# Staging two chunks of the values' weights in another tile at the start of the second layer

## The chip, the cores and the metric

The kernel runs on one core of one Trainium2 chip. The metric is the device time of one execution in microseconds; the median of several runs is compared. Engines are named as in the profile: PE (TensorE, matrix products), DVE (VectorE), ACT (ScalarE), POOL (GpSimd) and SP, which issues all transfers here.

## The reference

Two layers, each of a linear attention and a dense part, with the same weights in both layers. All data is float32, x has 2048 rows of 640.

```
x = A_x
x = x + attention(layernorm(x), wqkv, w_phi, wo)
x = x + mish_mlp(layernorm(x), w1, b1, w2)
x = x + attention(layernorm(x), wqkv, w_phi, wo)
x = x + mish_mlp(layernorm(x), w1, b1, w2)

attention: q, k, v = split(x @ wqkv)            # 32 heads of 20
           pq, pk = q @ w_phi, k @ w_phi        # per head
           phi(p) = [softmax(p), softmax(-p)]
           kv, z  = phi_k^T v, sum of phi_k
           (phi_q kv) / (phi_q z + 1e-6) @ wo
mish_mlp:  h = x @ w1 + b1                      # 640 -> 1536
           (h * tanh(softplus(h))) @ w2         # 1536 -> 640
```

## The kernel before

**Products.** Every float32 operand of a large product is split into a high and a low part in a rounded float32 format, and each product is done three times: high by high, high by low, low by high. For a weight the split is `split` (lines 136 to 138) or `make_parts` (156 to 159): ACT copies the raw chunk into the high part, and DVE or POOL subtracts that from the raw chunk for the low part. A raw chunk is 128 rows of the weight, so a weight of 640 rows has five chunks, `k` = 0 to 4.

**Stages.** The 2048 rows go in eight blocks of 256, `b` = 0 to 7. Each layer has three stages. `attend_first` projects keys (`k0`, `k1`), values (`v0`, `v1`) and queries (`q0`, `q1`) of both 128-row halves of a block with `project_half` (line 364), and sums the keys' features times the values into one PSUM tile (line 436). `attend_second` applies the sums to the queries and projects with `wo` (also line 364). `dense` does the two products with Mish between them: `hidden` (line 759), `mish` (772 to 785, which ends with the high and low parts `ol` of the activation), `contract` (line 801, two steps behind `hidden`), and `end` (819 to 829: adds the residual, writes the rows out, normalises them for the next layer and spills the transposed rows to DRAM as `n_d`, line 337).

**The switch of layers.** In layer one's `dense`, the last pass of the loop (`i == len(steps) - 1`, line 870) calls `load_v_weights` (183 to 188) for layer two: the columns `D` to `2 * D` of the tiles `r1h`, `r1l` get the values' weights again, from the input `wv`. The same tiles held `w1` until the last `hidden`. The keys' weights, folded with `w_phi` in layer one and kept in DRAM (`wp_d`), are fetched into the other columns (line 200), and the queries' weights into `r2h`, `r2l` (line 194). Just ahead of it the loop takes the first block of layer two, `nxt`: its transposed rows were loaded by `load_turned` (line 345) into two tiles of values and one tile of rows, and `nxt.all()` (lines 305 and 306) splits them into `xth` and `xtl`. In layer two `b == 0` has the order `v0`, `k0`, `k1`, `v1`, `q0`, `q1`. The values of the first block go into single PSUM tiles (`one`, four in all, of which one holds the sum over the keys), two for each half of 128 rows; keys and queries go into the double tiles `mm` (two in all), which `contract` holds till `end`.

**Tiles between.** A raw chunk of `wv` goes through a tile that belongs to something else at other times. `fetch_v` (line 177) takes for `k` = 0 and 1 a tile of normalised rows (`xn`, tag of four buffers), for 2 and 3 a tile of values (`v`, two buffers), and for 4 a tile of the Mish steps (`big`, five buffers). The tile of a block's rows (`xt`, made by `x_tile`, two buffers, 128 by 2 by 640) holds a block of the residual stream: `dense` fetches the next block's rows into one while the other is in use, and the last use of one is in `end`. In the second layer `attend_first` has no use for it.

**Order.** Except where a part is written out by hand, a planner sets the order of the instructions on each engine's queue at build time, from times that it reckons and from the program's order; on the chip each queue then runs in that order, and waits where an input is not there. `issue_after` queues what is in it behind a given instruction of the same engine: so the splits of `load_v_weights` stand on ACT behind the last exponential of `mish`, and `act` (line 123) queues each of its copies behind the one before it in the program. The splits of the output weights for layer two (`make_five`, line 208, its transfers at line 151, its copies at line 158) are not held in that chain.

Of the kernel before, what the change touches and what calls it, by code (L numbers as in the profile page):

```python
# [16 lines left out]
P = 128  # L17
S = 2048
D = 640
# [22 lines left out]
def kernel(  # L42
# [13 lines left out]
    nc = tc.nc  # L56
# [17 lines left out]
    def x_tile():  # L74
        return work.tile([P, BT, D], F32, tag="x", name="xt", bufs=2)
# [17 lines left out]
    two = const.tile([P, 1], F32, name="two")  # L93
# [42 lines left out]
    def split(hi, lo, st):  # L136
        nc.scalar.activation(hi, st, AF.Copy)
        nc.vector.tensor_tensor(lo, st, hi.bitcast(F32), op=ALU.subtract)
# [26 lines left out]
    def r1_pair(k):  # L165
        return tuple(wts.tile([P, F], F32R, tag=f"r1{s}{k}", name=f"r1{s}{k}") for s in "hl")
# [10 lines left out]
    def fetch_v(k):  # L177

        st = (row_tile, row_tile, v_tile, v_tile, big_tile)[k]()[:, :D]
        nc.sync.dma_start(st, wv[k * P:(k + 1) * P, :])  # L180
        return st

    def load_v_weights():

        ws = [r1_pair(k) for k in range(KD)]
        for k in range(KD):
            split(ws[k][0][:, D:2 * D], ws[k][1][:, D:2 * D], fetch_v(k))
        return ws

    def load_q_weights():  # L190
# [554 lines left out]
    def dense(x_src, x_dst, w1s, w2s, first, last):  # L745
# [97 lines left out]
        for i in range(len(steps) + SKEW):  # L843
# [26 lines left out]
            if i == len(steps) - 1 and not last:  # L870
                with tc.issue_after(exps[0]):
                    kv_ws = load_v_weights()
# [90 lines left out]
```

## Time and profile before

| | us |
|---|---|
| median of three runs | 1378.19 |
| lowest, highest | 1376.71, 1378.69 |
| the profiled execution's own time | 1376.81 |
| its span, from the first to the last instruction | 1375.0 |
| PE, weight loads busy | 1362.1, 1349.8 |
| DVE, ACT, POOL busy | 1073.3, 581.3, 441.0 |
| mean granted clock of PE | 0.999 |

The profile is of one execution. A row of the timeline gives start and length in us, engine (SPq is SP's queue of transfers), line, operation, tile written and tiles read, and in brackets the idle time of the engine before it and what ended it; `x3` says that three instructions stand in the row. Weight loads and products of PE overlap, and a product's end is modelled. Names like `in_wv` and `in_wo` are the inputs in DRAM.

### The profile page before, as it was taken

The page shows a single profiled execution, that of the slowest core. Times are in us where ns is not written, and L with a number is a line of the kernel's source. Part 1 is how long each engine was busy: PE and PEld are TensorE (multiplying, and loading weights), DVE is VectorE, ACT ScalarE, POOL GpSimd, SP SyncE. Part 2 cuts the span into 40 slices and gives each one's busy share as a digit, 9 for nine tenths or more (in the row PEclk, how much of TensorE's full clock was granted, in tenths as well). Part 3 has the DMA queues.
Part 4 walks back from the last instruction along what each step waited for, and adds up shares of the span by engine and source line. Part 5 has one row for each costly group of instructions (what it writes and reads, how often), then busy time and mean ns, then how long its engine had stood idle before and what let it go on. Part 6 is the DMA issues. An engine that isn't in the chain of part 4 may idle for free.

```text
span 1375.0 us, 30860 instructions
## 1 busy us (share of the span) xinstructions
PE 1362.1 (99%) x12896; PEld 1349.8 (98%) x12896; DVE 1073.3 (78%) x1822; ACT 581.3 (42%) x970; POOL 441.0 (32%) x334
## 2 busy tenths in 40 slices
PE   9999999999999999999999999999999999999998
PEld 8999999999999999999999999999999999999998
DVE  5898877886688887788769899988678776677775
ACT  4344443222454545545444334332235444454443
POOL 1345553354322222122235434444242111111112
PEclk9999999999999999999999999999999999999999
DMA  9443424788614442244473433368975221333200
GB/s 337 148 95 62 75 40 96 204 242 292 224 55 97 116 105 77 59 107 99 141 245 77 85 59 64 67 132 270 285 253 151 77 59 41 94 97 96 69 29 20
DMA packets 350469, 169.85 MB, mean 124 GB/s; under 512 B 287209, under 2 KB 323801, under 8 KB 350329
## 3 DMA queue, kind: packets, MB, share of 16 engines
q1 hardware_dynamic: 350329, 167.88, 45.2%
q8 instruction: 101, 1.65, 0.5%
q14 instruction: 39, 0.32, 0.1%
HBM read 104.92 MB, written 62.91 MB: 122 GB/s over the span
## 4 chain that ended last, share of the span: by engine, by line
PE 96%; DMA 1%; DVE 1%; ACT 0%; issue 0%; DVEq 0%; SPq 0%
PE mm L364 29%; PE one L759 24%; PE mm L801 24%; PE one L364 12%; PE mm L637 3%; PE one L300 2%; PE one L436 2%; DMA v<-in_wv 1%; DMA r1l<-wp_d 0%; DVE r1l L251 0%; DVE bn L270 0%; ACT xn L129 0%; DVE r L397 0%; DVE xt L811 0%; ACT r L129 0%
## 5 line engine op out<-in xcount | busy, mean ns | idle before, releaser
L801 PE MATMUL mm<-r2h,ol 128*128 128x320 f32 x1280 | 305.0, 309 | 0.0
L785 POOL TENSOR_TENSOR ol<-big,ol 128x512 fp32r<-128x512 f32 (+1 forms) x98 | 129.9, 1326 | 483.7 <-ACT ol L784 409.3
L759 PE MATMUL one<-xtl,r1h 128*128 128x256 f32 x960 | 268.2, 279 | 0.0
L759 PE MATMUL one<-xth,r1l 128*128 128x256 f32 x960 | 268.0, 279 | 0.0
L759 PE MATMUL one<-xth,r1h 128*128 128x256 f32 x960 | 265.9, 279 | 0.0
L801 PEld LDWEIGHTS mm<-r2h,ol 128*128 128x128 f32 x1280 | 219.2, 188 | 0.3 <-ACT ol L784 0.3
L801 PE MATMUL mm<-r2l,ol 128*128 128x320 f32 x640 | 197.3, 309 | 0.0
L364 PE MATMUL mm<-r1h,xth 128*128 128x320 f32 x600 | 187.6, 313 | 1.6 <-DVE r1l L251 1.6
L364 PE MATMUL mm<-r1l,xth 128*128 128x320 f32 x600 | 185.8, 310 | 0.0
L364 PE MATMUL mm<-r1h,xtl 128*128 128x320 f32 x600 | 185.6, 310 | 0.0
L759 PEld LDWEIGHTS one<-xtl,r1h 128*128 128x128 f32 x960 | 180.4, 188 | 0.0
L759 PEld LDWEIGHTS one<-xth,r1l 128*128 128x128 f32 x960 | 180.4, 188 | 0.0
L759 PEld LDWEIGHTS one<-xth,r1h 128*128 128x128 f32 x960 | 179.6, 188 | 0.0
L774 DVE TENSOR_SCALAR big<-big 128x512 f32<-128x512 f32 (+1 forms) x98 | 57.1, 583 | 110.0 <-ACT big L772 109.8
L399 POOL TENSOR_TENSOR r<-r,r 128x1280 f32<-128x1280 f32 x32 | 77.7, 2429 | 156.4 <-DVE r L398 141.8
L801 PEld LDWEIGHTS mm<-r2l,ol 128*128 128x128 f32 x640 | 120.2, 188 | 0.0
L776 ACT ACTIVATE big<-big,two 128x512 f32<-128x512 f32 (+1 forms) x98 | 70.1, 716 | 116.1 <-DVE big L775 116.0
L772 ACT ACTIVATE big<-one,b1s 128x256 f32<-128x256 f32 x192 | 80.9, 468 | 89.0 <-PE one L759 88.5
L784 ACT ACTIVATE ol<-big 128x512 fp32r<-128x512 f32 (+1 forms) x98 | 60.9, 622 | 136.0 <-DVE big L783 135.9
L364 PEld LDWEIGHTS mm<-r1h,xth 128*128 128x128 f32 x600 | 112.8, 188 | 2.6 <-DVE r1l L251 1.8
L364 PEld LDWEIGHTS mm<-r1h,xtl 128*128 128x128 f32 x600 | 112.7, 188 | 0.2
L364 PEld LDWEIGHTS mm<-r1l,xth 128*128 128x128 f32 x600 | 112.8, 188 | 0.0
(133 smaller groups left out, 3119.9 us busy)
## 6 DMA issues: line engine op xcount, KB each, us to landing
e_d<-r SPq DMA_DIRECT2D x128, 160.0 KB, 4.0
big<-e_d SPq DMA_DIRECT2D x32, 640.0 KB, 7.6
x_d<-xt SPq DMA_DIRECT2D x23, 640.0 KB, 3.9
xt<-x_d SPq DMA_DIRECT2D x22, 640.0 KB, 5.5
n_d<-xn SPq DMA_DIRECT2D x176, 80.0 KB, 2.2
xt<-in_x SPq DMA_DIRECT2D x16, 640.0 KB, 4.4
xn<-x_d SPq DMA_DIRECT2D x28, 320.0 KB, 4.4
v<-n_d SPq DMA_DIRECT2D x30, 256.0 KB, 3.1
```

Source lines behind the costliest of these rows:

```text
L300: nc.tensor.transpose(ps[:, c, t * P:(t + 1) * P], self.rows[t][:, (c0 + c) * P:(c0 + c + 1) * P], ident)
L364: nc.tensor.matmul(ps[:, :HC], a[:, sl], r, start=(k == 0 and n == 0), stop=(k == KD - 1 and n == 2))
L399: nc.gpsimd.tensor_tensor(eg, eg, r.unsqueeze(2).to_broadcast([P, 2 * H, DH]), op=ALU.mult)
L436: nc.tensor.matmul(kva[32 * j:32 * j + DH + 1, 40 * r:40 * r + 40], v[:, (DH + 1) * h:(DH + 1) * (h + 1)], e[:, 40 * h:40 * h + 40], start ...
L637: nc.tensor.matmul(po[64 * q:64 * q + 64, c, GW * j:GW * j + w], phs[g][:n, s0:s0 + 64], kvb[:n, g, :w], start=True, stop=True)
L759: nc.tensor.matmul(ph[:, j, :], l, r, start=(n == 0), stop=(n == 3 * KD - 1))
L772: exps[0] = nc.scalar.activation(part(ta, 0)[:, j - js.start], ph[:, j, :], AF.Exp, bias=b1s[:, 2 * pr + j:2 * pr + j + 1]).ins
L774: nc.vector.tensor_scalar_min(e, e, E_CAP)
L776: nc.scalar.activation(r, n, AF.Ln, bias=two)
L784: nc.scalar.activation(ah[:, js], n, AF.Copy)
L785: nc.gpsimd.tensor_tensor(al[:, js], n, ah[:, js].bitcast(F32), op=ALU.subtract)
L801: nc.tensor.matmul(pys[t][:, c, :HC], l[:, j, sl], r, start=(f == 0 and n == 0), stop=(f == KF - 1 and n == 2))
```

## The change

For the second layer, chunks 2 and 3 of `wv` are fetched into the two halves of one tile of a block's rows, and split from there. Chunks 0, 1 and 4 go through the same tiles as before. The first layer, which calls `fetch_v` itself, is unchanged.

```diff
     def load_v_weights():
 
         ws = [r1_pair(k) for k in range(KD)]
+        two = x_tile()
         for k in range(KD):
-            split(ws[k][0][:, D:2 * D], ws[k][1][:, D:2 * D], fetch_v(k))
+            if k in (2, 3):
+                st = two[:, k - 2]
+                nc.sync.dma_start(st, wv[k * P:(k + 1) * P, :])
+            else:
+                st = fetch_v(k)
+            split(ws[k][0][:, D:2 * D], ws[k][1][:, D:2 * D], st)
         return ws
```

## The prediction

> **What bounds the kernel now.** I read the page first (busy times, then the chain that ended last), then the list of who waited for whom on TensorE, and then only the switch from layer one to layer two, around 690 us, because that is where the edited function runs: the chain within that window, the busy times there, and the timelines of the queues.
>
> ```profile
> PE 1362.1 (99%) x12896; PEld 1349.8 (98%) x12896; DVE 1073.3 (78%) x1822; ACT 581.3 (42%) x970; POOL 441.0 (32%) x334
> ...
> PE 96%; DMA 1%; DVE 1%; ACT 0%; issue 0%; DVEq 0%; SPq 0%
> ```
>
> TensorE is the bound: 1362.1 of 1375.0 us, and 96% of the chain. Everything that can be won in the whole span is 12.9 us of idle TensorE. In the list of its waits (total, times, longest, in us) one row belongs to this change:
>
> ```profile
> PE one L364 <- ACT r1h L137: 0.9, 1, 0.9
> ```
>
> A projection (L364) waits for a cast of line 137, which is `split` of a chunk of the values' weights, once. The chain through the switch shows which chunk (start, length, what):
>
> ```profile
> 695.81 7.14 DMA v<-in_wv
> ...
> 702.97 0.74 ACT r1h L137
> ...
> 703.76 0.71 PE one L364 x3
> 704.47 1.17 PE mm L801 x8
> 705.64 3.52 PE one L364 x24
> 709.16 8.80 PE mm L364 x60
> 717.96 2.20 PE one L364 x15
> ```
>
> Chunk 2 goes through a tile of values: its transfer starts at 695.81, lands after 7.14 us, is cast in 0.74, and TensorE starts at 703.76. After that TensorE is never late until the second attention: one product takes 8.80/60 = 0.147 us, and 60 and 15 follow at that pace.
>
> ```profile
> 690.00:697.00 7.00, 7.00 (x51) 7.00 (x50) 5.10 (x13) 5.32 (x12) 1.29 (x1) 1.00 0.95 336
> 696.00:700.00 4.00, 4.00 (x29) 4.00 (x28) 3.12 (x8) 1.89 (x5) 2.03 (x1) 1.00 1.03 404
> 697.00:705.00 8.00, 7.05 (x46) 6.53 (x45) 4.87 (x10) 3.02 (x6) 2.76 (x2) 1.00 0.79 295
> 705.00:718.00 13.00, 13.00 (x91) 13.00 (x90) 5.56 (x13) 5.74 (x11) 7.31 (x7) 1.00 0.52 172
> ```
>
> Those are busy times by stretch (length, then PE, PEld, DVE, ACT, POOL, granted clock, DMA share, GB/s). Only the stretch from 697 to 705 has a hole: 8.00 - 7.05 = 0.95 us of products, 8.00 - 6.53 = 1.47 us of weight loads. The clock is 1.00 throughout, so it plays no part.
>
> **The change part by part.** Two transfers of 320 KB, two casts and two subtractions stay as they are; only the tile between them differs. Nothing is added to the work of any engine. What moves is when the two transfers may start, and with them the order of four instructions. The transfer queue, SP:
>
> ```profile
> 668.54 0.34 SPq L825 DMA_DIRECT2D x_d<-xt  x1
> ...
> 674.99 7.01 SPq L337 DMA_DIRECT2D n_d<-xn  x8
> ...
> 683.57 0.43 SPq L180 DMA_DIRECT2D xn<-in_wv  x1
> ...
> 695.81 2.90 SPq L180 DMA_DIRECT2D v<-in_wv  x2
> ```
>
> *Start of the transfers.* The two v transfers stand behind the two casts and subtractions (`step`, L305 and L306) that empty the tiles of values into `xth` and `xtl`; these run after the last exponentials of layer one. The free tile of rows is the one of block 6. It is last read by its write-out at 668.54 and by its normalising on ACT (next fence, 672.85, 1.72 long, so to 674.57). Block 7's own rows stand in the other. So the transfers may start from about 674.6, behind the spill of eight pieces, which ends at 682.00, if the planner puts that first: 13.8 us earlier than 695.81 at the worst. SP waits for nothing new; behind them on SP would be the spill and the reloads of the queries' weights, each by 2 x 0.43 = 0.86 us, and the queries come last in the block.
>
> *The transfers themselves.* The DMA engines are full already (0.95 and 1.03 of them busy). One chunk of 327,680 bytes at the 404 GB/s of the fullest stretch is 0.81 us. Two go ahead of all that is queued from 684 on, so the fifth chunk, the one in `big`, would land up to 1.62 us later: it was there at 699.06, and would be at 700.7. With a cast of 0.74 and a subtraction of 0.82 it would be ready at 702.3, against 705.4 (703.74 + 1.63, below) for the last of the v chunks now. So the set of five is complete 3.1 us earlier, and the fifth chunk is late next. TensorE begins the values at 697.39:
>
> ```profile
> 697.39 0.60 PE L364 MATMUL one<-r1h,xth 128*128 128x320 f32 x3
> ...
> 717.80 0.31 PE L364 MATMUL one<-r1h,xth 128*128 128x320 f32 x1
> ```
>
> From there it has 36 products on chunks 0 to 3 (four chunks, three products, the three halves of values that have a PSUM tile) before it must touch the fifth, 5.3 us; with half of the last 24 products of the dense stage between them (1.8 us) that is 704.5, so it does not wait for the fifth. The Trainium skill, "DMA: Bandwidth & Descriptors", section Queues, rings and completion order, says that each DMA engine consumes its descriptors in ring order; that rule speaks against the change, and by it the 1.62 us of delay falls on the fifth chunk in full. No run here shows the new order yet.
>
> *Casts and subtractions.* On ACT:
>
> ```profile
> 672.85 1.72 ACT L129 ACTIVATE xn<-xt,stats 128x640 f32<-128x640 f32 x2
> ...
> 699.06 0.74 ACT L137 ACTIVATE r1h<-big 128x640 fp32r<-128x640 f32 x1 [1.89 <-DMA big<-in_wv]
> ...
> 714.26 0.74 ACT L158 ACTIVATE r2h<-raw 128x640 fp32r<-128x640 f32 x1 [3.90 <-DMA raw<-in_wo]
> 714.90 1.73 ACT L129 ACTIVATE xn<-xt,stats 128x640 f32<-128x640 f32 x2
> ...
> 716.65 0.74 ACT L129 ACTIVATE v<-one 128x320 f32<-128x320 f32 x2
> ...
> 734.18 0.74 ACT L158 ACTIVATE r2h<-xn 128x640 fp32r<-128x640 f32 x1 [4.46 <-DMA xn<-in_wo]
> ```
>
> The hole of 1.89 us ahead of 699.06 holds the two casts (2 x 0.74 = 1.48), so they cost ACT nothing if they fall there. The two subtractions have no such place (DVE's timeline from 701 on, and the row of POOL's in the same time):
>
> ```profile
> 701.03 0.43 DVE L783 SCALAR_TENSOR_TENSOR big<-big 128x256 f32<-128x256 f32 x1
> 703.74 1.63 DVE L138 TENSOR_TENSOR r1l<-v,r1h 128x640 fp32r<-128x640 f32 x2 [2.28 <-ACT r1h L137]
> 701.99 0.73 POOL L785 TENSOR_TENSOR ol<-big,ol 128x256 fp32r<-128x256 f32 x1 [2.36 <-ACT ol L784]
> ```
>
> They now stand after L783, the last DVE step of the dense stage; put ahead of it they delay that stage's last `ol` by 0 to 1.63 us. It is ready at 702.72 now (701.99 + 0.73); its last eight products ran only from 704.47 behind the late chunk, so 1.75 us of cover is there, and I take nothing for it.
>
> *The sum.* The wait of line 364 goes. Lower end 0.78 us: next in line is the PSUM slot for the fourth half of the values. The copy that frees it starts at 716.65 and its first half ends about 717.02, and TensorE's 15 products for that half come at 717.80 (second row of TensorE's timeline above); if the copy stays where it is, TensorE can come only 0.78 us earlier. Upper end 1.47 us, the weight loads' hole. The hole of products, 0.95, lies between. I take the middle, 1.1 us. [...]
>
> The profiled execution took 1376.81 us, 1.81 around its span of 1375.0, and 1.38 under the 1378.19 of the runs' median. So the same kernel profiled should show 1376.81 - 1.1 = 1375.7, and the median of runs 1378.19 - 1.1 = **1377.1 us**, 0.08% less. About 0.2% (2.76 us) is what a measurement of this kernel can tell from no change, so this is no change.
>
> **The rivals.**
>
> *Given back (1378.2 us).* The planner puts the two subtractions and casts ahead of the last steps of the dense stage, the last `ol` comes up to 1.63 us later, and TensorE waits for that instead of for the chunk; or the values' copy on ACT, which `act` holds behind the normalising of block 7, keeps its place and eats the rest. For it: DVE is 5.10 of 7.00 busy before 697, without a hole of 1.63. Against: 1.75 us of cover. The gain of 1.1 goes to nothing or little.
>
> *Slower (1381.5 us).* One mechanism, on ACT's queue. The copy of the values at 716.65 stands in program order behind the normalising of block 7 at 714.90, and that behind a cast of the output weights at 714.26 which waited 3.90 us for its transfer. These casts (L158) are free for the planner to place; it places them by reckoned times, and the change moves those times. One more of them in front, the fifth, costs as at 734.18: 4.46 of waiting and 0.74 of cast, 5.20 us. The slack before TensorE notices is 0.78. So the last half of values starts 5.20 - 0.78 = 4.4 us later than now if the queue in front of the copy keeps its place, and 3.3 us later if it comes the 1.1 us earlier with the end of the dense stage. I take the second: 1378.19 + 3.3 = 1381.5. It decides as soon as the copy ends over 0.78 us later. For it: the slack is that small, and the queues in front are in order. Against: the order after 705 follows from the dense stage's end, which hardly moves. A second step displaced would double it.
>
> *Faster by over 0.2%.* It would take 2.76 us of idle TensorE, and from 690 to 718 there are at most 1.47 us; the rest of the 12.9 lies in stretches that the edited function does not run in. Only a new order in the attention behind could bring it: about 1375 us.
>
> *It does not do what it says:* the tile of block 6 is held longer than I read, and the transfers stay near 695.8. Then nothing changes, and it counts with "given back".
>
> **How the numbers follow.** My forecast 0.38, given back 0.22, slower 0.34, faster 0.06. The first two lie within 0.2%: 0.60. I give the slower case that much because four in-order queues are laid out anew by reckoned times around a slack of 0.78 us, where the gain is limited to 1.47. The forecast's own range is 1378.19 - 1.47 = 1376.7 to 1378.19 - 0.78 = 1377.4. The range for 8 in 10 starts 1 us under that for the noise of the median (the three runs spread over 1.98), at 1375.7, and must take in most of the slower case: its price and a good part of a second step, to 1383.0.
>
> **What would show it.** Right: in the profile after, the transfers into `xt` from `in_wv` start before 684; the row of L364 waiting for the cast of L137 is gone or names `big`; TensorE's 60 products of L364 into `mm` start at about 708 instead of 709.16; weight loads from 697 to 705 are over 7.5 of 8.00; and the `v<-one` copy comes at 716 or before. Wrong: a wait of TensorE of over 1 us on `v<-one` or on `ol` between 697 and 725; a cast of L158 with a long wait for `in_wo` standing newly before the values' copy; or a difference in a stretch that the change cannot reach.

## The result, and the profile after

The changed kernel takes 1380.31 us (median of 22 runs, 1378.15 to 1384.43) against 1377.82 us for the kernel before (22 runs, 1376.62 to 1380.38). The ratio is 1.0019 [1.0013, 1.0025]: slower by 0.19%, 2.5 us between the medians. The forecast was 1377.1. The profiled execution took 1380.52 us, its span is 1378.7; both lie 3.7 us above those of before. Line numbers behind the edited function are 6 higher than before (line 364 is 370, 783 is 789, 306 is 312).

From the page, and from the list of TensorE's waits (total, times, longest, in us):

```profile
PE 1363.5 (99%) x12896; PEld 1351.0 (98%) x12896; DVE 1075.1 (78%) x1822; ACT 580.7 (42%) x970; POOL 442.9 (32%) x334
...
PE one L306 <- issue: 1.8, 1, 1.8
PE one L370 <- ACT v L129: 1.6, 1, 1.6
...
PE mm L370 <- DVE xtl L312: 1.0, 2, 0.7
```

The wait of 0.9 us for the cast of line 137 is gone, as forecast. In its place stand a wait for the copy of the values and two waits for `xtl`, the low part of a block's turned rows. Neither row is in the list of before. (The first row belongs to the start of the second attention, near 936 us; before, the wait there is 0.7 us.) The stretches that the prediction showed (length, PE, PEld, DVE, ACT, POOL, granted clock, DMA share, GB/s):

```profile
690.00:697.00 7.00, 7.00 (x51) 7.00 (x50) 5.22 (x13) 5.47 (x11) 1.27 (x1) 1.00 1.03 399
...
697.00:705.00 8.00, 8.00 (x56) 8.00 (x56) 4.96 (x9) 2.33 (x6) 3.29 (x2) 1.00 0.75 278
705.00:718.00 13.00, 11.63 (x78) 11.10 (x76) 4.29 (x11) 4.49 (x7) 7.34 (x8) 1.00 0.49 168
```

From 697 to 705 the hole is closed: 8.00 of weight loads where there were 6.53. The next stretch, full before, has a hole of 1.37 us of products and 1.90 us of weight loads. Timelines of TensorE, SP, ACT, DVE and POOL there (start, length, engine, line, operation, tiles; in brackets the idle time before and what ended it):

```profile
705.49 0.31 PE L370 MATMUL one<-r1h,xtl 128*128 128x320 f32 x1
705.64 0.31 PE L807 MATMUL mm<-r2h,ol 128*128 128x320 f32 x1
...
707.25 0.31 PE L807 MATMUL mm<-r2h,ol 128*128 128x320 f32 x1
707.89 0.41 PE L370 MATMUL mm<-r1h,xth 128*128 128x320 f32 x1 [0.33 <-DVE xt L825]
...
674.84 0.36 SPq L190 DMA_DIRECT2D xt<-in_wv  x1
...
683.54 0.53 SPq L190 DMA_DIRECT2D xt<-in_wv  x1
...
694.92 0.33 SPq L180 DMA_DIRECT2D big<-in_wv  x1
...
702.60 5.65 SPq L151 DMA_DIRECT2D raw<-in_wo  x3
...
701.49 0.74 ACT L137 ACTIVATE r1h<-big 128x640 fp32r<-128x640 f32 x1 [3.32 <-DMA big<-in_wv]
703.91 0.42 ACT L790 ACTIVATE ol<-big 128x256 fp32r<-128x256 f32 x1 [1.69 <-DVE big L789]
...
715.73 0.74 ACT L158 ACTIVATE r2h<-raw 128x640 fp32r<-128x640 f32 x1 [3.46 <-DMA raw<-in_wo]
716.37 1.72 ACT L129 ACTIVATE xn<-xt,stats 128x640 f32<-128x640 f32 x2
...
718.12 0.74 ACT L129 ACTIVATE v<-one 128x320 f32<-128x320 f32 x2
...
697.56 1.54 DVE L138 TENSOR_TENSOR r1l<-xt,r1h 128x640 fp32r<-128x640 f32 x2
...
699.96 0.41 DVE L787 SCALAR_TENSOR_TENSOR big<-big 128x256 f32<-128x256 f32 x1
702.26 0.83 DVE L138 TENSOR_TENSOR r1l<-big,r1h 128x640 fp32r<-128x640 f32 x1 [1.89 <-ACT r1h L137]
703.00 0.42 DVE L788 SCALAR_TENSOR_TENSOR big<-big 128x256 f32<-128x256 f32 x1
703.45 0.42 DVE L789 SCALAR_TENSOR_TENSOR big<-big 128x256 f32<-128x256 f32 x1
...
704.41 0.74 POOL L791 TENSOR_TENSOR ol<-big,ol 128x256 fp32r<-128x256 f32 x1 [3.43 <-ACT ol L790]
```

Read TensorE's rows first. Before the change, its last eight products of the dense stage ran from 704.47 to 705.64. Now the last twelve run from 705.64 to 707.56. Counted from the last product of `hidden` in each profile (690.24 before, 690.12 after), the stage ends at 17.44 us instead of 15.40, 2.0 us later. TensorE does not wait for that: up to 707.56 no row from 697 on has a wait in brackets. Its queue, which the planner lays out like the others, has another order. Before, 21 products of the values stood ahead of the last eight products of the dense stage; now 45 do.

DVE's rows show that the activation is late as well. The two subtractions of the moved chunks (1.54 us) stand ahead of the last three steps of Mish, lines 787 to 789. Between 787 and 788 stands the subtraction of the fifth chunk, as it stood between 781 and 782 before:

```profile
699.84 0.82 DVE L138 TENSOR_TENSOR r1l<-big,r1h 128x640 fp32r<-128x640 f32 x1 [0.81 <-ACT r1h L137]
```

Then DVE waited 0.81 us for it. Now the chunk's transfer is issued at 694.92 instead of 692.30, its cast comes at 701.49 instead of 699.06, and DVE stands idle for it for 1.89 us with the last two Mish steps queued behind. The last `ol` is ready at 704.41 + 0.74 = 705.15 instead of 702.72. But TensorE takes it up only at 705.64, so this lateness does not hold TensorE up. In five more profiles with the same place of the last twelve products (e2, e4, e10, e11 and e15 below), `ol` is ready 0.7 to 1.8 us before they start, and they start 15.51 us after the last of `hidden` in all of them.

With the last product of the dense stage the whole end of the layer moves. SP issues three transfers of the output weights from 702.60 on and stands 9.1 us in all for products of the dense stage (`SPq L151 <- PE mm L807`; 6.6 before), which free the tiles; the row of the three ends at 708.25 instead of 706.33. Four casts of the output weights stand on ACT ahead of the normalising, in both profiles. The last of them comes at 715.73 instead of 714.26, the normalising at 716.37 instead of 714.90 and, in ACT's order behind that, the copy of the values at 718.12 instead of 716.65: from the last of `hidden`, 1.6 us later. TensorE goes on 0.47 us after the start of that copy (718.59), so the slack before was 717.80 - 716.65 - 0.47 = 0.68 us, where the prediction had 0.78, and 0.9 us are lost. TensorE is 1.4 us earlier than before at 703, waits 0.33 us at 707.56 for the residual that frees `mm`, and then 1.6 us for the copy.

The second loss is 70 us further on, in the first block of layer two, where the edited function does not run. The write-out of the second query tile (SP, line 448 or 454), ACT's copy of a later query projection into the slot that it frees, the DVE step that waits for this copy, and the last `xtl` of the next block. Before, then after:

```profile
753.66 3.77 SPq L448 DMA_DIRECT2D e_d<-r  x4
...
760.33 0.71 ACT L129 ACTIVATE r<-mm 128x640 f32<-128x640 f32 x1 [4.72 <-DMA e_d<-r]
...
761.07 1.54 DVE L388 TENSOR_REDUCE m<-r 128x32 f32<-128x640 f32 x2 [0.23 <-ACT r L129]
...
784.70 1.50 DVE L306 TENSOR_TENSOR xtl<-xn,xth 128x256 fp32r<-128x256 f32 x1
```

```profile
754.67 4.46 SPq L454 DMA_DIRECT2D e_d<-r  x4
...
762.82 0.71 ACT L129 ACTIVATE r<-mm 128x640 f32<-128x640 f32 x1 [4.77 <-DMA e_d<-r]
...
763.55 0.82 DVE L394 TENSOR_REDUCE m<-r 128x32 f32<-128x640 f32 x1 [3.34 <-ACT r L129]
...
787.70 1.49 DVE L312 TENSOR_TENSOR xtl<-xn,xth 128x256 fp32r<-128x256 f32 x1
```

The copy waits for the landing of a write to DRAM. It comes 2.49 us later, DVE idles 3.34 us for it in one piece, and `xtl` starts 3.00 us later and is ready at 789.19. That is past the point where TensorE wants it. Besides being shifted by the switch, block 0's steps stand in a new order: the planner, reckoning with other times, put both keys' maxima first on DVE, and on POOL the subtraction of the first query's maxima (line 395) ahead of the multiplication of the first key's features (line 405). TensorE's order of products in this block differs too. Differences in the queues are confined to the switch and this block.

One table follows TensorE through all of it. It gives how much later (+) or earlier (-) than in the profile of before TensorE begins the same product, counted from the last product of `hidden` in layer one, which removes what executions differ by before the switch (-1.1 to +1.6 us). The columns are times in the profile of before; the experiments' names are those below. The next to last column is the start of ACT's copy behind the write-out, counted from the same product (70.09 before); the last, the total of TensorE's waits for `xtl`.

| profile | 703 | 725 | 780 | 830 | 945 | copy at | `xtl` |
|---|---|---|---|---|---|---|---|
| after | -1.38 | +1.01 | +0.68 | +2.22 | +3.88 | 72.69 | 1.0 |
| e10 (after) | -1.38 | +0.95 | +0.62 | +2.15 | +3.13 | 72.95 | 1.0 |
| e11 (after) | -1.38 | +0.91 | +0.58 | +2.20 | +4.03 | 72.86 | 1.0 |
| e1 | +0.08 | +0.08 | -0.25 | -0.25 | +0.18 | 69.89 | 0 |
| e8 | +0.14 | +0.15 | -0.18 | -0.18 | +0.49 | 69.84 | 0 |
| e12 | -0.36 | -0.36 | -0.69 | +1.04 | +3.02 | 71.79 | 1.2 |
| e7 | +0.22 | +0.37 | +0.04 | +2.09 | +3.21 | 72.63 | 1.5 |
| e2 | -1.38 | +1.06 | +1.06 | +1.06 | +1.60 | 71.55 | 0 |
| e4 | -1.38 | +1.08 | +1.09 | +1.08 | +3.10 | 71.88 | 0 |
| e6 | -1.38 | +0.07 | +0.07 | +0.07 | +0.64 | 70.66 | 0 |
| e3 | -1.38 | -0.81 | -0.79 | -0.63 | +0.55 | 69.75 | 0 |
| e5 | -1.38 | -0.77 | -0.76 | +0.80 | +4.03 | 71.51 | 1.0 |
| e13 | +0.54 | +0.54 | +0.54 | +0.54 | +1.28 | 67.94 | 0 |
| e14 | +0.38 | +0.38 | +0.05 | +0.05 | +0.82 | 67.46 | 0 |
| e15 | -1.38 | +3.24 | +2.91 | +2.91 | +3.67 | 70.79 | 0 |

Two rows hold something else besides. In e15 the granted clock is 0.84, 0.50 and 0.80 in the three stretches of 2 us from 720 on, and in e5 it is 0.57 from 937 to 941. The share that is missing, times the length, gives 1.7 us each time (an estimate), in the columns 725 and later for e15 and in the column 945 for e5.

### The profile page after: what moved, and what is told of

It is laid out like the page before. It is cut to its first block, busy times and chain, and to the rows that moved or that the text cites. A ratio compares the mean times of both kernels' runs of the same rounds, so it can differ in the third digit from the quotient of the medians.

```text
span 1378.7 us, 30858 instructions
## 1 busy us (share of the span) xinstructions
PE 1363.5 (99%) x12896; PEld 1351.0 (98%) x12896; DVE 1075.1 (78%) x1822; ACT 580.7 (42%) x970; POOL 442.9 (32%) x334
## 5 line engine op out<-in xcount | busy, mean ns | idle before, releaser
L807 PE MATMUL mm<-r2h,ol 128*128 128x320 f32 x1280 | 304.9, 309 | 0.0
L807 PEld LDWEIGHTS mm<-r2h,ol 128*128 128x128 f32 x1280 | 219.2, 188 | 0.0
L807 PE MATMUL mm<-r2l,ol 128*128 128x320 f32 x640 | 197.3, 309 | 0.0
L807 PEld LDWEIGHTS mm<-r2l,ol 128*128 128x128 f32 x640 | 120.2, 188 | 0.0
```

What stands on the lines that cost most here:

```text
L807: nc.tensor.matmul(pys[t][:, c, :HC], l[:, j, sl], r, start=(f == 0 and n == 0), stop=(f == KF - 1 and n == 2))
```

## The experiments

Two theories stood at the start. *Switch*: the loss is the subtractions and the late fifth chunk ahead of Mish's last steps, which make the dense stage end late. *Order*: the loss is the new order of block 0's steps on DVE and POOL. Where a kernel needs a given order of those steps, they are chained with dependencies that add no wait: the names below are maxima (M), minima (N), subtractions (S, D), sums (R), reciprocals (C), multiplications (P).

**e1: the kernel before with the new order of block 0.**

```diff
+                chain("Mk0 Nk0 Mk1 Nk1 Sk0 X0b0 Sk1 Dk0 Dk1 Rk0 X1b0 Mq0 Nq0 ...")   # DVE, as after
+                chain("Sq0 Pk0 Sq1 Pk1")                                             # POOL, as after
```

> The kernel before, with one thing of the changed one: the DVE and POOL steps of block 0 of layer two (maxima, subtractions, sums, reciprocals of the features, from the second key tile on) are chained in the order that the planner gave them after the change; transfers, tiles and the switch stay as before. Theory Q (that order costs the time behind 718 us): slower than before by 1.5 to 2.9 us, about 1380, with TensorE waits near 790 and 820 us and the first kv product of layer two at about 735 instead of 731. Theory S (the late end of the dense stage costs everything, and the later waits are its echo): within 0.5 us of before, no wait near 790.

Measured: 1380.6 us (11 runs, 1376.47 to 1381.66) against 1377.28, ratio 1.0019 [1.0010, 1.0027]. The order alone costs as much as the whole change. TensorE's order of products moved with it, from 731 to 740 us, so its part is not separated from that of DVE and POOL. But the profile, of an execution that took 1376.47, shows no wait for it. The order seems to cost in some executions only.

**e2: the changed kernel with the old order of block 0.**

```diff
+                chain("Mk0 Nk0 Sk0 Mk1 Nk1 Dk0 X0b0 Sk1 Rk0 Dk1 X1b0 Ck0 Mq0 Nq0 ...")   # DVE, as before
+                chain("Pk0 Sq0 Pk1 Sq1")                                                 # POOL, as before
```

> The changed kernel, with the same DVE and POOL steps of block 0 of layer two chained in the order that they had before the change; the two chunks still go through the tile of rows. Theory Q: only the switch's own balance is left, 1.5 us gained at 703 and 2.4 us lost by 718, so about 1 us over before, 1378.8, the wait for the values' copy near 717 still there. Theory S: as the changed kernel, 1380.3, with the waits near 790 and 820.

Measured: 1378.5 us (1377.52 to 1380.13), 1.0006 [0.9997, 1.0014]. What is left of the loss is the switch: +1.06 at 725 in the table, and no more of it up to 830. The wait for the copy of the values (1.7) is still there. In the runs this rest is not clear of the noise: the interval takes in 1.

**e3: as e2, with the subtractions of chunks 2, 3 and 4 behind Mish's last DVE step.**

```diff
-            split(ws[k][0][:, D:2 * D], ws[k][1][:, D:2 * D], st)
+            with tc.issue_after(step) if k in (2, 3, 4) else nullcontext():
+                split(ws[k][0][:, D:2 * D], ws[k][1][:, D:2 * D], st)
```

> As the run before this one, and the three subtractions for the low parts of chunks 2, 3 and 4 queued on DVE behind the last DVE step of Mish. Theory S in its form that DVE's queue made the dense stage end late (two subtractions of 0.8 us ahead, and the fifth chunk's, which waits for its transfer, in front of two steps of Mish): the last activation part is ready near 703 instead of 705.1, the wait for the values' copy near 717 goes, and the time is 0.5 to 1.5 us under before, 1376.5 to 1377.3. If ACT's queue holds it instead (its copy of the fifth chunk, landing near 701.5, stands ahead of the last activation too), it is ready near 703.5 at best and the time is that of before, 1377.5 to 1378.3.

Measured: 1377.65 us (1376.45 to 1381.78), 1.0003 [0.9994, 1.0013]. The timelines and TensorE's list of waits:

```profile
700.92 1.29 POOL L809 TENSOR_TENSOR ol<-big,ol 128x256 fp32r<-128x256 f32 x1 [2.25 <-ACT ol L808]
...
715.47 0.74 ACT L129 ACTIVATE v<-one 128x320 f32<-128x320 f32 x2
...
PE one L371 <- ACT v L129: 0.4, 1, 0.4
```

The last `ol` is ready at 702.21, and the copy of the values starts at 715.47; TensorE waits 0.4 us for it. Its lead of 1.38 us shrinks only to 0.8, and this holds to 830. So with the subtractions held the switch loses nothing, and a gain of 0.8 us is there; it does not show in the median, which missed the expected 1376.5 to 1377.3. The edit changed TensorE's order too: 30 products of the values stand ahead of the last eight of the dense stage, not 45, and the stage ends at 15.24 us after the last of `hidden`, not at 17.44 as in e2. TensorE waits for `ol` neither here nor in e2. So, as the traces read, the subtractions act through the order that the planner gives TensorE, and not through time that TensorE spends waiting for them.

**e4: as e2, with the two transfers into `xt` issued behind the fifth chunk's.**

```diff
+        got = nc.sync.dma_start(st4, wv[4 * P:5 * P, :]).ins
+        for k in (2, 3):
+            with tc.issue_after(got):
+                nc.sync.dma_start(two[:, k - 2], wv[k * P:(k + 1) * P, :])
```

> The changed kernel with block 0's steps in the old order, and the two transfers into the tile of rows issued behind that of the fifth chunk, as late as they were before the change. So only the tile is changed and the freedom of the tiles of values. If the early transfers (which put the fifth chunk 2.4 us back) are the cause at the switch: the fifth chunk is there by 699.5 and the time is within 0.6 us of before, 1377.2 to 1378.4. If the tile itself or the queue order at the switch costs: slower than before by over 1 us.

Measured: 1379.35 us (1377.21 to 1384.17), 1.0014 [1.0003, 1.0024]. The switch loses the same 1.08 as in e2. The early transfers are not what costs, and neither is a late landing of the fifth chunk: its cast comes 8.6 us after the last of `hidden`, against 8.8 before the change and 10.7 in e2. What e4 shares with e2 is TensorE's order at the end: the last twelve products start at 15.51.

**e5: as e3, with ACT's copy of the fifth chunk behind Mish's last copy too.**

```diff
-            with tc.issue_after(step) if k in (2, 3, 4) else nullcontext():
+            with tc.issue_after(step) if k in (2, 3, 4) else nullcontext(), tc.issue_after(copy) if k == 4 else nullcontext():
```

> As the changed kernel with the three subtractions behind the last DVE step of Mish and block 0's steps in the old order, and besides ACT's copy of the fifth chunk queued behind Mish's last copy. So neither queue holds the dense stage's end for the late fifth chunk. Theory S: the last product of the dense stage comes 14.0 to 15.0 us after the last of line 759's (15.1 before, 17.1 after the change), the wait near 717 is gone, and the gain of about 1 us that was forecast is there: 1376.0 to 1377.0, under before. If the late landing of the fifth chunk then makes TensorE itself wait (values' products on it), 0.5 to 1.5 us come back there and the time is that of before.

Measured: 1377.47 us (1375.96 to 1380.72, 12 runs), 1.0001 [0.9992, 1.0009]; the expected 1376.0 to 1377.0 was missed. The switch is as in e3, with the same order on TensorE. The profiled execution was the slowest of its runs and shows waits for `xtl` (1.0 us) although block 0 stands in the *old* order. That is what brought the theory of the order down in its first form: the order is not needed for that wait.

**e6: as e5, but only the fifth chunk is held; the subtractions of chunks 2 and 3 stay ahead of Mish's steps.**

```diff
-            with tc.issue_after(step) if k in (2, 3, 4) else nullcontext(), tc.issue_after(copy) if k == 4 else nullcontext():
+            with tc.issue_after(step) if k in (4,) else nullcontext(), tc.issue_after(copy) if k == 4 else nullcontext():
```

> As the run before this one, but only the fifth chunk's copy and subtraction are held behind Mish's last steps; the subtractions of chunks 2 and 3 stand ahead of Mish's last DVE steps, as in the changed kernel. If the fifth chunk is what makes the dense stage end late, this has most of the gain: the end of the dense stage 15.0 to 15.9 us after the last of line 759's, 1376.3 to 1377.5. If the two subtractions (1.54 us) are what does it: 16.5 us and over, the wait near 717 back, 1378.0 to 1379.0.

Measured: 1378.33 us (1376.76 to 1381.46), 1.0008 [0.9999, 1.0017]. By the bounds set for it, this is the second case, that of the two subtractions: the dense stage ends at 16.56 us after the last of `hidden`, and the wait near 717 is back with 1.3 us. At 725 the table has +0.07, between e2 (+1.06, nothing held) and e5 (-0.77, all held). So in this order of holding, the fifth chunk is worth about 1.0 us of the switch's loss and the two subtractions 0.8. Both go through TensorE's order again: here 39 products of the values stand ahead of the last eight, and `ol` is ready at 12.85 us, 2.4 before these start.

**e7: the kernel before with POOL's part of the new order only; e9: with DVE's part only.** Against e1:

```diff
-                chain("Mk0 Nk0 Mk1 Nk1 Sk0 X0b0 ...")   # e7: DVE as before
+                chain("Mk0 Nk0 Sk0 Mk1 Nk1 Dk0 ...")
...
-                chain("Sq0 Pk0 Sq1 Pk1")                # e9: POOL as before
+                chain("Pk0 Sq0 Pk1 Sq1")
```

> The kernel before, with only POOL's four feature steps of block 0 in the order that they have after the change (the subtraction of query tile 0 ahead of the multiplication of key tile 0, and the same for tile 1); DVE keeps the old order. If POOL's order is what costs in the earlier run with both orders (3.3 us there): 1379.0 to 1380.6, the first kv product of layer two over 3 us later than before. If DVE's order does it: 1377.0 to 1378.0.

> The kernel before, with only DVE's steps of block 0 of layer two chained in the order that the changed kernel has (maxima of both keys first); POOL's four steps there keep the order of before. If the +0.19% of the run with both new orders comes from DVE's part, this reads 1.0015 to 1.0022. If it comes from neither alone but from the two together, 1.0000 to 1.0006. If that +0.19% came only from a larger share of late executions drawn by chance, it reads under 1.0008 with a median under 1378.5. In the profile, the stage from the last product of hidden to the last product of the dense stage stays at 15.1 to 15.3 us under every theory.

Measured: e7 1377.92 us (1376.03 to 1379.3), 1.0000 [0.9992, 1.0009]; e9 1382.31 us (1381.56 to 1384.47, 5 runs), 1.0041 [1.0027, 1.0054]. e7's number speaks for DVE's part by its bounds; but its profile, of the slowest of its runs, has a wait for `xtl` of 1.5 us with POOL's order alone. e9 met none of its expectations, because the two queues no longer fit. From its DVE timeline and list of waits:

```profile
740.60 0.82 DVE L404 TENSOR_TENSOR r<-m,r 128x640 f32<-128x640 f32 x1 [6.22 <-POOL r L402]
...
PE mm L365 <- ACT r L129: 4.3, 1, 4.3
```

DVE reaches the query's step early and stands 6.22 us for POOL's subtraction, which is queued behind a multiplication; the write-outs come 5 us later, and TensorE waits 4.3 us for the copy into the freed slot. So e9 says nothing on DVE's share of the 0.19%. It shows the same path to TensorE, by accident, with a larger delay; and behind that wait the granted clock is 0.50 from 761 to 764 us.

**e8 and e12: the kernel of e1 twice more, for its profile.**

> A second profile of the kernel before with block 0's DVE and POOL steps in the new order; its first profile caught an execution of 1376.5 us, the fastest of eleven, whose median was 1380.6. Theory Q: this one is above 1379 and shows TensorE waiting for xtl of DVE between 780 and 830 us, as the changed kernel's did. If it is slow and shows no such wait, the order's price lies elsewhere.

> The kernel before with block 0's steps on DVE and POOL in the new order, a third profile (the first two caught executions of 1376.5 and 1378.0, without a TensorE wait between 780 and 830 us). If the new order is what makes such waits possible, an execution at 1380 or more shows waits for xtl (L307) near 787 or 817 us of 1 to 2 us, and one under 1378.5 shows none. If the late executions are late for another reason, one at 1380 or more shows no such wait and loses its time elsewhere.

Measured: 1378.02 and 1378.69 us. e8 shows no wait for `xtl`; e12 shows one of 1.2 us, and the path to it. The write-out, ACT's copy behind it and DVE's step behind that, in e8 and then in e12:

```profile
753.44 3.89 SPq L461 DMA_DIRECT2D e_d<-r  x4
...
760.53 0.70 ACT L129 ACTIVATE r<-mm 128x640 f32<-128x640 f32 x1 [3.72 <-DMA e_d<-r]
...
761.27 0.82 DVE L401 TENSOR_REDUCE m<-r 128x32 f32<-128x640 f32 x1 [2.28 <-ACT r L129]
```

```profile
752.77 4.27 SPq L461 DMA_DIRECT2D e_d<-r  x4
...
760.92 0.70 ACT L129 ACTIVATE r<-mm 128x640 f32<-128x640 f32 x1 [4.78 <-DMA e_d<-r]
...
761.65 0.82 DVE L401 TENSOR_REDUCE m<-r 128x32 f32<-128x640 f32 x1 [3.31 <-ACT r L129]
```

Same program, same queues. Counted from the last product of `hidden` (690.68 in e8, 689.13 in e12), the first of the four transfers is issued at 62.8 and 63.6, and the copy comes at 69.8 and 71.8. DVE then waits 1.0 us longer in e12. The expectation had tied the wait to executions of 1380 or more; e12 took 1378.69 with it, having begun the switch 1.5 us earlier than e8. The stage shows the wait; the total does not tell.

**e10 and e11: the changed kernel twice more.**

> The changed kernel once more, for a second profile. Fixed losses by the order of the queues: the dense stage ends 17.1 us after the last product of hidden, and TensorE waits 1.5 to 1.8 us for the copy of the values (L129), as in the first profile. Losses that come in some executions only: the waits for the subtraction of xtl near 787 and 817 us (1.0 and 0.7 there) and the idle time at the start of the second attention may be absent; then the time is about 1378. If they belong to the order and not to the execution, they are there again and the time is about 1380.5.

> As the look before it: the dense stage's end at 17.1 us and the wait for the values' copy of 1.5 to 1.8 us again under every theory; the waits near 787 and 817 us again (1380.5) if they belong to the order, absent (about 1378) if they belong to the single execution.

Measured: 1379.99 and 1380.49 us. Both have both losses: 1.6 and 1.5 us for the values' copy, 1.0 us for `xtl`. The wait near 817 of the first profile is absent as a row, though 0.2 to 0.4 us still go there.

By now a new theory, *write-out*: the switch shifts block 0 by a microsecond, and the new order brings its write-outs later, so that the landing of the second one passes the point, some 71.5 us after `hidden`, from which DVE's chain to `xtl` is late for TensorE. In the table the wait stands in each profile with the copy at 71.79 or later except e4 (71.88, where TensorE itself comes 1.1 us late); of the two near 71.5 it stands in e5, where TensorE comes 0.8 us early, and not in e2, where it comes 1.1 us late. With TensorE's own lateness at 780 taken off the column of the copy, the rows part cleanly: 72.0 to 72.6 where the wait stands, 67.4 to 70.8 where it does not. Its rival: DVE's new order costs by itself, and the landing only goes with it.

**e13, e14, e15: a quarter of that write-out, in the kernel before, in e1's kernel and in the changed kernel.** The other 30 of the 40 column groups are left out.

```diff
-                nc.sync.dma_start(dst[t, q], e[32 * q:32 * q + 32].rearrange("f (j s) -> f j s", s=32))
+                n = 10 if layer and i == 1 else 40
+                nc.sync.dma_start(dst[t, q][:, :n], e[32 * q:32 * q + 32].rearrange("f (j s) -> f j s", s=32)[:, :n])
```

> The kernel before; of the features of the second query tile of block 0 of layer two only 10 of 40 column groups are written out (40 KB instead of 160 KB in each of four transfers), everything else and every queue's order stays. This is the landing that ACT's copy of the next query projection waits for. Theory of the write-out: the late executions go, so the median falls to 1376.3 to 1377.2 (ratio 0.9993 to 0.9999), and DVE's idle time near 761 us falls from 1.2 to 4.1 us to under 1. Rival (what is late is DVE itself, by its order): no change, 1.0000 within 0.0005.

> The kernel before with block 0's DVE and POOL steps in the new order, and the same smaller write-out. Theory of the write-out: the new order costs only because it brings the landing to the edge where TensorE waits near 787 us, so without it the ratio falls from 1.0019 to within 0.0004 of the kernel before with the small write-out, about 1377. Rival (the order costs by itself): 1.0015 to 1.0022, about 1380.5, as with the full write-out.

> The changed kernel (its queues in the order it has) with the same smaller write-out. Theory of the write-out: the waits near 787 and 817 us go and the fixed loss at the switch stays (dense stage ends 17.1 us after hidden, 1.5 to 1.8 us of waiting for the copy of the values): about 0.9 us over the kernel before with the small write-out, 1377.8 to 1378.4, ratio 1.0004 to 1.0008. Rival (the order costs by itself): 1380 or more, 1.0018.

Measured, against 1377.87 for the kernel before (27 runs): e13 1377.51 us (11 runs, 1376.57 to 1381.29), 1.0002 [0.9993, 1.0011]; e14 1376.97 us (1375.73 to 1380.54), 1.0001 [0.9992, 1.0009]; e15 1377.94 us (1376.83 to 1381.15), 0.9999 [0.9990, 1.0008]. The new order, 1.0019 with the full write-out, costs nothing that can be measured with the small one, and neither does the change. (e1 and e14 ran on two different chips, each beside the kernel before.) e15's ACT timeline and its longest wait at the switch:

```profile
761.61 0.70 ACT L129 ACTIVATE r<-mm 128x640 f32<-128x640 f32 x1 [0.84 <-DMA e_d<-r]
...
PE one L370 <- ACT v L129: 2.3, 1, 2.3
```

The copy now waits 0.84 us for the landing instead of 4.77, and the wait for `xtl` is gone, in an execution that stood 3.24 us late behind the switch, some 1.7 of it by the low clock, and was the slowest of its runs. A late TensorE alone would have hidden a late `xtl`; but with its lateness at 780 taken off as above, the copy stands at 67.9, far from the 72.0 where waits stand. The rival expected 1.0015 or more for e14 and 1.0018 for e15, and it falls. Two things went otherwise than expected: the kernel before gains nothing that can be measured from the small write-out, probably because its landing is seldom late; and e15 reads a little under its 1.0004 to 1.0008, so the switch's loss of 0.9 us cannot be told from nothing in the medians. In e13 to e15 one small load of `e_d` also moved ahead of two loads of `n_d` on SP, behind the write-out in e14 and e15 and ahead of it in e13.

No version beat the kernel before. e3 and e5, which keep the gain at the switch, read 1.0003 and 1.0001.

## Why the prediction was wrong

**What held.** The transfers into `xt` start at 674.84 and 683.54, before 684. The wait for the cast is gone, the 60 products into `mm` start at 707.9, and weight loads from 697 to 705 are full. TensorE's lead at 703 is 1.38 us, inside the 0.95 to 1.47 that the holes gave and close to the weight loads' end. The Trainium skill, "Perfetto Trace Analysis", section Identifying the Most-Contended Engine, takes busy weight loads, and not busy products, as the measure of how close TensorE is to its limit; the lead of 1.38 against holes of 1.47 and 0.95 agrees with this. Two of the signs of being wrong came true: the wait on the copy of the values, 1.6 us, and a difference in a stretch "that the change cannot reach".

**The step that failed: the end of the dense stage, for which the sum says "I take nothing" and which "hardly moves".** It moved by 2.0 us. The text weighed only how late the last `ol` could be (at most 1.63 us against 1.75 of cover) and left TensorE's own order of products as it was. In the new build that order has 45 products of the values ahead of the last eight of the dense stage instead of 21. The stage's end follows this number in the experiments: 15.24 us after the last of `hidden` with 30 products ahead (e3, e5), 16.56 with 39 (e6), 17.44 with 45 (e2, e4 and after), at the 0.147 us for a product that the prediction itself had. From there the 2.0 us reach the copy of the values as 1.6, of which 0.7 was slack; 1.0 us is lost at 725 where about 1.1 was to be won.

Why the planner chose this order is not on record. It changes when the three subtractions are held (e3, e5, e6), so the late `ol` in the planner's reckoning is the likely reason. No run has the change with TensorE's order of before.

Two more terms were off. The cover of 1.75 us was the wait that the change removes: once TensorE no longer stands for the late chunk, it is 1.4 us earlier, and the cover is 0.4. Had its order stayed, an `ol` that is 2.4 us late would have stopped it; that is argued, not run. And the fifth chunk was asked only whether TensorE waits for it. It does not; DVE does, with Mish's steps behind. The delay of its transfer was undersized: 2.43 us at the cast (701.49 against 699.06), not 1.62, because its issue on SP moved by 2.62. Counted from the last of `hidden`, the cast comes 2.5, 1.6 and 1.2 us later in the three profiles of the changed kernel, so this varies from one execution to the next.

**The rivals.** "Given back" foresaw a late `ol`, which came, and a wait of TensorE for it, which did not; its other branch, the values' copy behind the normalising of block 7, is what holds TensorE, with a price that stopped at the gain. In fact 1.38 won became 0.91 to 1.01 lost at 725. "Slower" named that copy too, with 0.78 of slack, and the casts of the output weights that stand ahead of it. But no fifth cast was put in front: four stand there in both profiles, and the later ones come late because their transfers stand behind the last products of the dense stage. That its number, 1381.5, lies nearer to the result than the forecast is in part luck, for half or more of the loss comes further on.

**What was not in the sum at all.** The larger part of the loss comes in a stretch "that the change cannot reach": 1.5 us from 780 to 830 and 1 to 2 us more up to 945. The last rival allowed a new order in the attention as a gain only. e1 shows that the new order in block 0, TensorE's included, costs 0.19% without the change, and e14 and e15 that this goes through one write-out. From 830 to 945 the profiles with a wait for `xtl` lose 1.8 us on average (1.0 to 3.2, of which e5's 3.2 holds 1.7 of low clock) and the others 0.8 (0.1 to 2.0, e9's 0.1 included). The largest single wait there is at the start of the second attention, near 936 us: 0.7 us before, and 0.9 to 2.0 in thirteen of the profiles, with a wait for `xtl` and without. So it is not shown that this part follows from the late chain. How the 2.5 us between the medians split is therefore open between two ends: by e2 some 0.8 to 1.2 us are the switch, by e15 nearly none.

## What to carry to other kernels

Look at the order of the bound engine itself in both builds, not only at its waits: here TensorE ran without a wait and still ended a stage 2.0 us later, because other products had been put ahead. When a stall goes, take it out of every cover that rests on it: work "hidden by a wait of 1.75 us" has no cover left if that wait is what the change removes. Ask of a moved transfer who stands behind its consumer in each in-order queue, not only when TensorE needs the data. And where a planner lays out the queues from reckoned times, a change of a microsecond reorders steps far behind it; compare the queues there, and look for a landing or a slot that has little slack.

## What was not expected of the hardware

The write-out of features is slow for its size. In the kernel before, from 745 to 764 us:

```profile
DMA packets 11155, 2.09 MB, mean 110 GB/s; under 512 B 10432, under 2 KB 11152, under 8 KB 11152
```

Nearly all are pieces of under 512 bytes; the write-out's are 32 floats, 128 bytes. The DMA engines' share and rate in the changed kernel, in the last two columns of its busy times by stretch:

```profile
754.00:763.00 9.00, 9.00 (x121) 8.74 (x120) 5.86 (x6) 1.20 (x3) 6.15 (x3) 1.00 0.92 169
```

At 0.92 of their time they move 169 GB/s; at the switch, from 690 to 697, it was 399 at 1.03. The Trainium skill, "DMA: Bandwidth & Descriptors", section Why small descriptors are slow (HBM only), puts this down to a fixed cost of each packet; these rows agree in that small pieces move slowly, but they do not show why. Landing, from the issue of the last of four transfers to ACT's copy, took 3.43 to 5.97 us in the profiles with the full write-out, though the transfers are the same.

A wait of TensorE can be followed by a slow stretch that costs more. In e15, behind the wait of 2.33 us that ends at 719.98 (third number from the end: the granted clock):

```profile
718.00:720.00 2.00, 0.02 (x1) 0.02 (x1) 1.29 (x2) 2.00 (x5) 1.49 (x1) 1.00 0.04 13
...
722.00:724.00 2.00, 2.00 (x9) 2.00 (x9) 2.00 (x4) 0.84 (x3) 0.00 (x0) 0.50 0.90 140
```

Nine products start in 2 us there instead of 15 or 16. The same stands in e9 behind its wait of 4.27 us, and in e5 behind one of 1.61 us at 936. But it does not stand behind the waits of 1.63 and 1.81 us in the changed kernel's profile or of 2.00 in e12, so the length of the wait alone does not decide it, and that the wait brings it is not shown. It is one reason why the same waits cost more in some executions than in others.

DVE and POOL also delay each other. The same DVE subtraction, in e8 and in e12, and POOL's subtraction of line 159 beside it:

```profile
738.24 0.81 DVE L402 TENSOR_TENSOR big<-big,m 128x640 f32<-128x640 f32 x1
...
738.27 2.20 POOL L159 TENSOR_TENSOR r2l<-xn,r2h 128x640 fp32r<-128x640 f32 x1
```

```profile
736.18 2.22 DVE L402 TENSOR_TENSOR big<-big,m 128x640 f32<-128x640 f32 x1
...
736.16 1.57 POOL L159 TENSOR_TENSOR r2l<-xn,r2h 128x640 fp32r<-128x640 f32 x1
```

Whichever starts first, by 0.03 or 0.02 us here, keeps its time (0.81, 1.57), and the other takes about that much longer (2.20, 2.22). The Trainium skill, "SBUF — State Buffer", section SBUF: two separate sides, states just that: a lock on a shared port pair, held for a whole instruction. In e12 DVE lost 1.4 us by it, in block 0, ahead of the write-outs: one way in which the same program lands them later in one execution than in another.
